# Pair 3 of a pooled attention kept in fp16 parts and transposed by DMA, with a new order of work

## The chip, the core and the metric

The kernel runs on one core of a Trainium2 chip. The metric is the device time in microseconds (us) of that core; three runs are shown for the kernel before, and their median is the figure that is forecast. TensorE's clock has two levels, 1.2 and 2.4 GHz; the profile gives the granted clock as a share of the upper one, so 0.50 is the lower level.

## The reference

The inputs q, k and v are (4 batches, 8 heads, 1152 rows, 64 columns), fp32, and the two weights are 512x2048 and 2048x512. Pooled attention comes first, then a feed-forward net with a squared ReLU:

```python
q_pool = q.reshape(B, H, S // 2, 2, D).mean(axis=3)          # 576 query rows
scores = scale * q_pool @ k.transpose(0, 1, 3, 2)            # 576 x 1152 per head
attn = exp(scores - max); attn = attn / (attn.sum(-1) + 1e-9)
x = (attn @ v).transpose(0, 2, 1, 3).reshape(2304, 512)
h = x @ w_in; g = relu(h) ** 2; out = g @ w_out              # fp32
```

## The kernel before

**Pairs and chunks.** Two heads make a pair; there are 16 pairs, four to a batch, so pairs 0 to 3 are batch 0. A pair has 9 chunks of 128 query rows, 144 chunks in all, numbered from 0. Pairs 2 and 3 are cut in two visits that alternate: chunks 18 to 21 and 26 to 30 are pair 2, chunks 22 to 25 and 31 to 35 are pair 3; pair 4 begins at chunk 36.

**The steps of a chunk i**, named as in the code: S.i are the scores (TensorE; lines 755 and 750 with fp16 parts, 734 in fp32), MX.i scales them and finds the row maximum (VectorE, DVE, line 766), MB.i forms the bias of the exponential, EX.i is the exponential with its row sum (ScalarE, ACT, line 790). Then the probabilities have to be transposed, in one of two ways:

- *fp32 by TensorE*: TP.i.x are three groups of three transposes through a PSUM bank (line 831), TC.i.x copies each group out (ACT line 841, or DVE line 843). The pair's values v are loaded as they are, and PV, the product with v, multiplies fp32 (line 942).
- *fp16 parts by DMA*: HI.i rounds to fp16 (ACT 794, DVE 798, POOL 363), LO.i is the rest (DVE or GpSimd, POOL, line 802), and TR.i is one transposing DMA for both parts (line 805, issued on SP's queue). The values are split too (VA and VD, DVE's part line 369), after a small Gram product GR and a norm GF that set their scale, and PV is 27 fp16 products for each head (line 950).

The setting FV lists the pairs of the first kind: 0, 1, 2 and 3 before.

**Preparing a pair n**: LK, LQ, LV (or LF, v as it is) load it on SP's queue; K and q are scaled and split (KA, KD, QA, QD) and transposed by DMA (KT line 628, QT line 641). QX.n.0 and QX.n.1 then copy the transposed q to the other half of the partitions (line 650, on DVE or POOL; a pair in the setting QXD has it moved by a plain DMA on SP's queue, line 647). Two raw buffers hold what is loaded.

**The feed-forward net.** Sixteen weight pieces are loaded (WL, UL), made into fp32 again (W0 to W5 and U0 to U5), and once the largest entry of w_out is known (US3.1, line 1316) split by WA (ACT, line 338), WB (ACT, line 1337) and WD (POOL, line 1341); for w_out these are UA, UB, UD. Nine blocks of 256 rows follow: RV, RB, XR divide by the row sums, XQ and XN find a norm, XA and XD split x (XA on ACT line 338, XD on DVE line 369), H.j.u are eight units of 24 matmuls with w_in (line 1114), HA, G1, G2, G3 the squared ReLU, O.j.t.d eight units of 12 matmuls with w_out (line 1163), OD and ST the output. The first block can begin as soon as batch 0's first rows have gone through PV.

**What sets the order.** Plan (line 50) takes every step with a fixed duration per engine, a priority (its place, plus an offset by kind from the tables off and off0 in CFG) and simulates five queues; the program is written out in the order that comes of it. Each engine, SP's queue too, then works its own list strictly in that order. So a step that waits holds up all that stands behind it on its engine.

Of the kernel before, what the change touches and what calls it, by code (L numbers as in the profile page):

```python
# [228 lines left out]
def kernel(  # L229
# [198 lines left out]
    def prep(n):  # L428
# [11 lines left out]
        def rk():  # L440
            return raw("k", n).rearrange("p (h c d) -> p h c d", h=2, c=9)
# [19 lines left out]
        if n == 0 and n in full_s:  # L461
            sk = k[b, 2 * hp : 2 * hp + 2].rearrange("h (p c) d -> p h (c d)", c=9)
            tk = rk

            def lk(o, x):
                nc.sync.dma_start(out=tk().rearrange("p h c d -> p h (c d)")[:, :, 192 * x : 192 * x + 192], in_=sk[:, :, 192 * x : 192 * x + 192])

            for x in range(3):
                add(("LK", n) + ((x,) if x < 2 else ()), {"SP": 900}, [], lambda o, x=x: lk(o, x), need, take=None if x else (("k", n), ("raw",), 0), after=[("LK", n, x - 1)] if x else prev)
        else:  # L470
            add(("LK", n), {"SP": 2500}, [], lambda o: load_kv(rk(), k), need, take=(("k", n), ("raw",), 0), after=prev)
        add(("LQ", n), {"SP": 2600}, [], load_q, need, take=(("q", n), ("raw",), 0), after=[("LK", n)])
# [980 lines left out]
```

## Time and the profile before

| | us |
|---|---|
| median of three runs | 796.63 (796.58 to 801.82) |
| the profiled execution, its own time | 804.16 |
| its span, first to last instruction | 802.3 |
| TensorE matmul busy in the span | 742.4 (93%) |
| DVE, ACT, POOL busy | 582.9 (73%), 575.4 (72%), 383.0 (48%) |
| mean granted TensorE clock | 0.977 |

The profiled execution is 7.5 us longer than the median; 1.9 us of its own time lie outside the span. A row of the list of groups reads: line, engine, operation, what it writes and reads with shape, count | busy us, mean ns of one | idle us of the engine before them and what ended it. A row of the timeline reads: start, us, engine, line, operation, count, and in brackets how long the engine had been idle and who released it. SPq is SP's queue: the time there is that of issuing a transfer, not of the transfer. Matmuls overlap, so the busy time of a group is less than count times mean.

### The profile page before, as it was taken

The page shows a single profiled execution, that of the slowest core. Times are in us where ns is not written, and L with a number is a line of the kernel's source. Part 1 is how long each engine was busy: PE and PEld are TensorE (multiplying, and loading weights), DVE is VectorE, ACT ScalarE, POOL GpSimd, SP SyncE. Part 2 cuts the span into 40 slices and gives each one's busy share as a digit, 9 for nine tenths or more (in the row PEclk, how much of TensorE's full clock was granted, in tenths as well). Part 3 has the DMA queues.
Part 4 walks back from the last instruction along what each step waited for, and adds up shares of the span by engine and source line. Part 5 has one row for each costly group of instructions (what it writes and reads, how often), then busy time and mean ns, then how long its engine had stood idle before and what let it go on. Part 6 is the DMA issues. An engine that isn't in the chain of part 4 may idle for free.

```text
span 802.3 us, 15287 instructions
## 1 busy us (share of the span) xinstructions
PE 742.4 (93%) x5998; PEld 491.7 (61%) x5998; DVE 582.9 (73%) x897; ACT 575.4 (72%) x894; POOL 383.0 (48%) x255
## 2 busy tenths in 40 slices
PE   4969788887899999998899999999999999999997
PEld 3546555544675577546666676577567657785654
DVE  3888999858799896888988899877888864202211
ACT  5776888778797888777897888788888854503412
POOL 2453633258676476365585656585666331001300
PEclk8888999999799999999999999999999999999999
DMA  8587383304999999999799999999999992000011
GB/s 285 207 218 214 119 239 136 75 9 90 219 187 202 192 227 210 211 209 183 159 212 210 207 207 208 211 201 213 204 209 199 182 189 46 1 1 14 14 27 27
DMA packets 324199, 127.77 MB, mean 159 GB/s; under 512 B 306976, under 2 KB 307744, under 8 KB 324128
## 3 DMA queue, kind: packets, MB, share of 16 engines
q1 hardware_dynamic: 324128, 126.80, 76.6%
q8 instruction: 47, 0.77, 0.4%
q14 instruction: 24, 0.20, 0.1%
HBM read 45.09 MB, written 4.72 MB: 62 GB/s over the span
## 4 chain that ended last, share of the span: by engine, by line
PE 42%; DVE 6%; DMA 4%; ACT 3%; issue 3%; POOL 1%; SPq 0%; ACTq 0%; DVEq 0%
PE ba L1163 9%; PE ba L1114 9%; PE bt L1163 6%; PE bt L1114 6%; PE s L755 5%; PE ba L950 5%; DVE s L766 2%; DMA PT<-buf 2%; DMA raw<-in_v_dram 1%; DVE region L1141 1%; ACT buf L794 1%; DMA kT<-buf 1%; PE s L750 1%; ACT buf L790 1%; DVE buf L802 1%
## 5 line engine op out<-in xcount | busy, mean ns | idle before, releaser
L766 DVE TENSOR_SCALAR_CACHE_REDUCE s<-s,esc 128x1152 f32<-128x1152 f32 x135 | 190.3, 1419 | 23.0 <-PE s L755 21.0
L1114 PEld LDWEIGHTS <-w 128*128 128x128 f16 x1728 | 169.1, 99 | 28.8 <-issue 3.2
L802 POOL TENSOR_TENSOR buf<-buf,buf 128x1152 f16<-128x1152 f32 x63 | 159.6, 2535 | 53.6 <-ACT buf L794 40.0
L790 ACT ACTIVATE buf<-s,ca 128x1152 f32<-128x1152 f32 x144 | 174.5, 1213 | 9.6 <-POOL ca L776 3.9
L755 PE MATMUL s<-kT,qT 128*128 128x512 f16 x720 | 136.6, 328 | 9.2 <-ACT buf L790 8.7
L1163 PE MATMUL ba<-w,region 128*128 128x512 f16 x624 | 142.3, 379 | 0.0
L1163 PEld LDWEIGHTS <-region 128*128 128x128 f16 x864 | 82.4, 98 | 95.6 <-issue 1.9
L1114 PE MATMUL ba<-region,w 128*128 128x256 f16 x1128 | 131.5, 274 | 1.2 <-DVE region L1041 0.5
L755 PEld LDWEIGHTS <-qT 128*128 128x128 f16 x720 | 64.0, 100 | 65.0 <-issue 16.5
L1141 POOL TENSOR_TENSOR region<-region 128x512 f16<-128x512 f32 x32 | 42.2, 1320 | 102.1 <-ACT region L1134 101.5
L950 PE MATMUL ba<-PT,v 128*64 128x320 f16 (+1 forms) x1296 | 84.7, 287 | 2.2 <-DMA PT<-buf 2.1
L794 ACT ACTIVATE buf<-buf 128x1152 f16<-128x1152 f32 x71 | 82.4, 1160 | 6.0 <-DMA PT<-buf 2.3
L950 PEld LDWEIGHTS <-v 128*64 128x64 f16 x1296 | 71.1, 110 | 15.0 <-issue 6.2
L802 DVE TENSOR_TENSOR buf<-buf,buf 128x1152 f16<-128x1152 f32 x45 | 67.5, 1501 | 16.2 <-ACT buf L794 11.6
L831 PE MATMUL ba<-ident,buf 128*128 128x128 f32 x324 | 51.6, 289 | 15.5 <-DVE PT L843 8.3
L1129 ACT ACTIVATE region<-region 128x512 f16<-128x512 f32 x72 | 45.0, 626 | 27.7 <-PE bt L1163 19.1
L1141 DVE TENSOR_TENSOR region<-region 128x512 f16<-128x512 f32 x40 | 39.1, 980 | 30.7 <-ACT region L1134 30.3
L831 PEld LDWEIGHTS ba<-ident,buf 128*128 128x128 f32 x324 | 35.2, 144 | 30.4 <-DVE PT L843 9.9
L1163 PE MATMUL bt<-w,region 128*128 128x512 f16 x240 | 52.6, 379 | 0.0
L1124 ACT ACTIVATE region<-ba 128x512 f32<-128x512 f32 x39 | 23.0, 591 | 36.8 <-PE ba L1114 36.8
L841 ACT ACTIVATE PT<-ba 128x384 f32<-128x384 f32 x74 | 34.0, 490 | 20.7 <-PE ba L831 20.0
L1114 PE MATMUL bt<-region,w 128*128 128x256 f16 x408 | 45.9, 273 | 0.0
(180 smaller groups left out, 993.9 us busy)
## 6 DMA issues: line engine op xcount, KB each, us to landing
raw<-in_q_dram SPq DMA_DIRECT2D x32, 288.0 KB, 3.7
raw<-in_k_dram SPq DMA_DIRECT2D x15, 576.0 KB, 4.6
region<-in_moe_w_in_dram SPq DMA_DIRECT2D x8, 1024.0 KB, 6.6
region<-in_moe_w_out_dram SPq DMA_DIRECT2D x8, 1024.0 KB, 5.3
raw<-in_v_dram SPq DMA_DIRECT2D x12, 576.0 KB, 4.7
out_dram<-half SPq DMA_DIRECT2D x20, 128.0 KB, 2.5
v<-in_v_dram SPq DMA_DIRECT2D x4, 576.0 KB, 7.1
out_dram<-buf SPq DMA_DIRECT2D x16, 128.0 KB, 2.4
```

Source lines behind the costliest of these rows:

```text
L755: nc.tensor.matmul(s[:, x, :w], lhsT=qt[:, l].rearrange("p c m -> p (c m)")[:, 128 * c0 + h : 128 * c0 + h + 255 : 2], rhs=rhs, **st)
L766: nc.vector.tensor_scalar(st3(), st3(), sc, 3e38, op0=ALU.mult, op1=ALU.min, accum_out=a[:, x : x + 1])
L790: nc.scalar.activation(P(), st3(), AF.Exp, bias=a[:, 1:2], scale=s1, accum_out=col)
L794: nc.scalar.activation(hl()[:, 0], P(), AF.Copy)
L802: e.tensor_tensor(out=hl()[:, 1], in0=P(), in1=hl()[:, 0], op=ALU.subtract)
L831: nc.tensor.matmul(t[:, y], lhsT=P()[:, c * 128 : (c + 1) * 128], rhs=ident, is_transpose=True, start=(y == 0), stop=(y == 2), skip_group_ ...
L841: nc.scalar.activation(out, t, AF.Copy)
L950: nc.tensor.matmul(px[h * 64 : (h + 1) * 64, 64 * r * (1 - h) : 64 * r * (1 - h) + N], lhsT=vv[:, h, kc, vl, :], rhs=p2(vi, r, h, 9 * pl + ...
L1114: nc.tensor.matmul(ph[:, f2], lhsT=w16[0][:, SLOT[f // 4], wl, a, f % 4 * 128 : (f % 4 + 1) * 128], rhs=xhl()[:, xl, a], start=(i == 0), s ...
L1129: nc.scalar.activation(gt[u][:, 0], rt[u % 2], AF.Square)
L1141: e.tensor_tensor(out=gt[u][:, 1], in0=rt[u % 2], in1=gt[u][:, 0], op=ALU.subtract)
L1163: nc.tensor.matmul(p[:, :DM], lhsT=g[:, gl, f % 2, tt * 128 : (tt + 1) * 128], rhs=w16[1][:, SLOT[f // 4], wl, f % 4], start=(f == 0 and g ...
```

## The change

FV loses pair 3, so pair 3 becomes one of the second kind: 27 TP and 27 TC go, and 9 HI, 9 LO, 9 TR, one VA, two VD, one GR, one GF come; LF.3 becomes LV.3, a load into a raw buffer. QXD, absent before, now lists pairs 1 to 4: their eight QX are plain DMAs. The fixed durations that Plan uses for SP's transfers and for LO on POOL are altered by up to 0.25 us each, and all offsets and slacks in CFG are new, so that every engine's list is in another order and some steps change their engine (KA is on POOL 9 times instead of 3, LO on POOL 70 times instead of 63, HI on ACT 87 times instead of 71).

```diff
-CFG = {'SPLIT': 0, 'TURN': [], 'TURNB': [], 'WDP': ((1, 0), (1, 1), (1, 2), (1, 3)), 'WSP': 0.3564, 'WOF': 20.8493, 'MSP': 9.2406, 'pen': 9140.9223, 'bl': 12.6041,
+CFG = {'SPLIT': 0, 'TURN': [], 'TURNB': [], 'WDP': ((1, 0), (1, 1), (1, 2), (1, 3)), 'WSP': 0.1233, 'WOF': 22.9195, 'MSP': 8.5588, 'pen': 10414.904, 'bl': 5.5869,
...
-'FV': (0, 1, 2, 3), 'FS': (0,), 'PART': 1,
+'FV': (0, 1, 2), 'FS': (0,), 'PART': 1, 'QXD': (1, 2, 3, 4),
...
-    ("WD", "DVE"): 2270, ("LO", "DVE"): 1285, ("LO", "POOL"): 2350, ("W4", "POOL"): 2120,
+    ("WD", "DVE"): 2270, ("LO", "DVE"): 1285, ("LO", "POOL"): 2420, ("W4", "POOL"): 2120,
...
-        add(("LQ", n), {"SP": 2600}, [], load_q, need, take=(("q", n), ("raw",), 0), after=[("LK", n)])
+        add(("LQ", n), {"SP": 2450}, [], load_q, need, take=(("q", n), ("raw",), 0), after=[("LK", n)])
...
-        add(("TR", i), {"SP": cfg("CTR", 2880)}, [("LO", i)] + ring, tr, i, give=("hl", i))
+        add(("TR", i), {"SP": cfg("CTR", 3010)}, [("LO", i)] + ring, tr, i, give=("hl", i))
```

**ACT's list up to XA.0**, the step that the first unit H.0.0 waits for. `w_1` and the scale `wS` are WA and WB of w_out, `PT<-ba` is TC, `s` the scores read by EX, `x_110` block 0. Before, the last twelve rows up to XA.0:

```order
L841 ACTIVATE PT<-ba_114 128x3x128
L1337 ACTIVATE region<-region,wS_1380 128x2048
L573 ACTIVATE buf_93,acc<-raw_101 128x576
L790 ACTIVATE buf_97,sums_87<-s_112,ca 128x1152
L794 ACTIVATE buf_96<-buf_97 128x1152
L338 ACTIVATE region<-ba_114 128x256
L338 ACTIVATE xm<-ba_114 64x64 x2
L338 ACTIVATE buf_93<-raw_101,psc 128x9x64
L338 ACTIVATE buf_95<-raw_102,psc 128x18x64
L1053 ACTIVATE half_100<-region 128x1024
L790 ACTIVATE buf_99,sums_87<-s_113,ca 128x1152
L338 ACTIVATE buf_97<-x_110,xs 128x1024
```

And now, from XQ of the same block to XA.0:

```order
L1053 ACTIVATE half_100<-x_110 128x1024
L790 ACTIVATE buf_95,sums_86<-s_112,ca 128x1152
L794 ACTIVATE buf_96<-buf_95 128x1152
L338 ACTIVATE w_1_91<-w_1_91,wS_1350 128x2048
L1337 ACTIVATE w_1_91<-w_1_91,wS_1350 128x2048
L338 ACTIVATE v_0_107<-raw_102,psc 128x18x64
L773 ACTIVATE ca<-ca,cols 128x1
L790 ACTIVATE buf_95,sums_86<-s_113,ca 128x1152
L794 ACTIVATE buf_97<-buf_95 128x1152
L338 ACTIVATE w_1_91<-region,wS_1350 128x2048
L338 ACTIVATE buf_99<-x_110,xs 128x1024
```

XA.0 now stands behind EX.35 and ahead of the last WB; before it stood behind EX.39, pair 4's fourth chunk, and behind the split of pair 5's q and K (the rows that read raw_101 and raw_102 with psc).

**SP's queue around the loads of pairs 4 and 5.** `raw<-in_q`, `in_k`, `in_v` are LQ, LK, LV, `qT` and `kT` QT and KT, `PT<-buf` a TR. Before, from LV.4 on:

```order
L450 DMA raw_101<-in_v_dram 128x2x576
L450 DMA raw_102<-in_k_dram 128x2x576
L641 DMA_TRANSPOSE qT_105<-half_100 128x9x128
L628 DMA_TRANSPOSE kT_103<-buf_99 128x18x128
L458 DMA raw_101<-in_q_dram 64x1152 x2
L805 DMA_TRANSPOSE PT<-buf_98 128x18x128
L805 DMA_TRANSPOSE PT<-buf_94 128x18x128
```

And now, from LQ.4 on:

```order
L458 DMA raw_102<-in_q_dram 64x1152 x2
L805 DMA_TRANSPOSE PT<-buf_96 128x18x128
L805 DMA_TRANSPOSE PT<-buf_97 128x18x128
L805 DMA_TRANSPOSE PT<-buf_95 128x18x128
L805 DMA_TRANSPOSE PT<-buf_94 128x18x128
L641 DMA_TRANSPOSE qT_105<-half_100 128x9x128
L450 DMA raw_102<-in_v_dram 128x2x576
L647 DMA qT_105<-qT_105 64x1152 x2
L450 DMA raw_101<-in_k_dram 128x2x576
L628 DMA_TRANSPOSE kT_103<-buf_96 128x18x128
L805 DMA_TRANSPOSE PT<-buf_99 128x18x128
```

QT.4, LV.4, QX.4, LK.5 and KT.4 now stand behind TR.22 to TR.25, pair 3's first four; QX.4 is on this queue and waits there for QT.4 to land.

## Rows read from the trace of the kernel before

**Rows 1.** Busy us by engine in five stretches, then clock, DMA share, GB/s.
```profile
core 0: us, PE busy (x) PEld busy (x) DVE busy (x) ACT busy (x) POOL busy (x), PEclk, DMA share, GB/s
0.00:80.00 80.00, 60.36 (x444) 41.16 (x445) 55.79 (x92) 53.50 (x85) 33.48 (x27) 0.87 0.76 231
80.00:157.00 77.00, 64.60 (x528) 42.61 (x528) 74.50 (x114) 63.86 (x101) 31.45 (x20) 1.00 0.51 149
157.00:206.50 49.50, 37.69 (x270) 21.59 (x267) 35.06 (x66) 40.19 (x53) 33.05 (x16) 0.89 0.35 67
206.50:660.00 453.50, 442.04 (x3760) 294.56 (x3761) 385.90 (x566) 371.23 (x586) 272.46 (x178) 0.99 1.07 202
660.00:802.00 142.00, 137.70 (x1006) 91.82 (x1004) 31.69 (x61) 46.66 (x75) 12.60 (x14) 1.00 0.10 21
```

**Rows 2.** The chain that ended last, a late piece.
```profile
787.34 10.37 PE bt L1163 x48
```

**Rows 3.** The list of groups: TensorE.
```profile
L831 PE MATMUL ba<-ident,buf 128*128 128x128 f32 x324 | 51.6, 289 | 15.5 <-DVE PT L843 8.3 <-ACT PT L841 4.8 <-ACT buf L790 1.9
L942 PE MATMUL ba<-PT,v 128*64 128x256 f32 (+1 forms) x288 | 38.4, 422 | 2.9 <-DVE x L1041 1.6 <-DVE wsc L1291 1.0
L950 PE MATMUL ba<-PT,v 128*64 128x320 f16 (+1 forms) x1296 | 84.7, 287 | 2.2 <-DMA PT<-buf 2.1
L547 PE MATMUL ba<-raw 128*128 128x128 bf16 x81 | 6.9, 236 | 6.8 <-DMA raw<-in_k_dram 6.4 <-ACT PT L841 0.5
```

**Rows 4.** The list of groups: ACT, DVE and POOL.
```profile
L841 ACT ACTIVATE PT<-ba 128x384 f32<-128x384 f32 x74 | 34.0, 490 | 20.7 <-PE ba L831 20.0
L843 DVE COPY PT<-ba 128x384 f32<-128x384 f32 x34 | 17.8, 551 | 2.2 <-PE ba L831 2.1
L794 ACT ACTIVATE buf<-buf 128x1152 f16<-128x1152 f32 x71 | 82.4, 1160 | 6.0 <-DMA PT<-buf 2.3 <-DMA kT<-buf 1.1
L802 POOL TENSOR_TENSOR buf<-buf,buf 128x1152 f16<-128x1152 f32 x63 | 159.6, 2535 | 53.6 <-ACT buf L794 40.0 <-DMA raw<-in_q_dram 5.7 <-issue 2.7
L802 DVE TENSOR_TENSOR buf<-buf,buf 128x1152 f16<-128x1152 f32 x45 | 67.5, 1501 | 16.2 <-ACT buf L794 11.6 <-POOL buf L802 2.4 <-POOL buf L363 1.5
L369 DVE SCALAR_TENSOR_TENSOR v<-raw,psc,v 128x576 f16<-128x576 f32 x24 | 36.3, 1518 | 0.5 <-POOL v L340 0.2
L650 DVE COPY qT<-qT 64x1152 f16<-64x1152 f16 x14 | 12.0, 860 | 2.7 <-DMA qT<-half 2.4
L766 DVE TENSOR_SCALAR_CACHE_REDUCE s<-s,esc 128x1152 f32<-128x1152 f32 x135 | 190.3, 1419 | 23.0 <-PE s L755 21.0 <-ACT buf L794 0.9 <-PE s L750 0.3
L790 ACT ACTIVATE buf<-s,ca 128x1152 f32<-128x1152 f32 x144 | 174.5, 1213 | 9.6 <-POOL ca L776 3.9 <-DVE s L766 2.9 <-DMA PT<-buf 0.9
```

**Rows 5.** Timeline of TensorE: the first H units.
```profile
206.56 4.05 PE L1114 MATMUL ba<-buf,w 128*128 128x256 f16 x24
...
211.43 5.40 PE L1114 MATMUL ba<-buf,w 128*128 128x256 f16 x48
```

**Rows 6.** Timeline of DVE and ACT: US3.1's end, UA.1.0, XA.0.
```profile
156.86 0.13 DVE L1316 TENSOR_SCALAR wsc<-wS 128x1 f32<-128x1 f32 x1
...
157.08 1.99 ACT L338 ACTIVATE w<-w,wS 128x2048 f16<-128x2048 f32 x1
...
198.55 1.15 ACT L338 ACTIVATE buf<-x,xs 128x1024 f16<-128x1024 f32 x1 [0.28 <-DVE xs L1082]
```

**Rows 7.** As rows 1, the stretch ahead of the first H.
```profile
192.00:208.00 16.00, 8.59 (x61) 4.75 (x58) 13.11 (x28) 12.04 (x19) 13.04 (x8) 0.72 0.96 177
```

**Rows 8.** Line 805 on SP's queue; a KT there; the S that followed.
```profile
L805 SPq DMA_TRANSPOSE PT<-buf x108: 2377/2858/4211, 192.8 to 660.4; - x108
...
493.64 4.15 SPq L628 DMA_TRANSPOSE kT<-buf  x1
...
501.40 1.14 PE L755 MATMUL s<-kT,qT 128*128 128x512 f16 x6 [0.26 <-DMA kT<-buf]
```

**Rows 9.** Timeline of DVE: a split beside an LO on POOL.
```profile
200.46 2.57 DVE L369 SCALAR_TENSOR_TENSOR buf<-raw,psc,buf 128x576 f16<-128x576 f32 x1
```

More of the change, by code (lines that the diff above doesn't have):

```diff
@@ L470, in prep @@
         else:
-            add(("LK", n), {"SP": 2500}, [], lambda o: load_kv(rk(), k), need, take=(("k", n), ("raw",), 0), after=prev)
-        add(("LQ", n), {"SP": 2600}, [], load_q, need, take=(("q", n), ("raw",), 0), after=[("LK", n)])
+            add(("LK", n), {"SP": 2350}, [], lambda o: load_kv(rk(), k), need, take=(("k", n), ("raw",), 0), after=prev)
+        add(("LQ", n), {"SP": 2450}, [], load_q, need, take=(("q", n), ("raw",), 0), after=[("LK", n)])
         if n in full_v:
-            add(("LF", n), {"SP": 2200}, oldv, lambda o: load_kv(v4(slot), v), visits[vs[0]][2], after=[("LQ", n)])
+            add(("LF", n), {"SP": 2250}, oldv, lambda o: load_kv(v4(slot), v), visits[vs[0]][2], after=[("LQ", n)])
         else:
-            add(("LV", n), {"SP": 2200}, [], lambda o: load_kv(rv(), v), need, take=(("v", n), ("raw",), 0), after=[("LQ", n)])
+            add(("LV", n), {"SP": 2250}, [], lambda o: load_kv(rv(), v), need, take=(("v", n), ("raw",), 0), after=[("LQ", n)])
         def qsum(o):
@@ L674, in prep @@
                 add(K + (h,), {"POOL": 1250} if kbp else {"DVE": 730}, [("KB" if kbp else "KA", n)] + ([K + (0,)] if h else []), lambda o, h=h: (kg if kbp else kd)(o, h), need, give=("k", n) if h else None)
-            add(("KT", n), {"SP": 2550}, [K + (1,)] + old, kt, need, give=("k2", n), take=(("kT", n), ("buf",), cfg("RK", 2)) if keep else None)
+            add(("KT", n), {"SP": 2700}, [K + (1,)] + old, kt, need, give=("k2", n), take=(("kT", n), ("buf",), cfg("RK", 2)) if keep else None)
             add(("QA", n), alt("QA", ACT=600, POOL=700), [("GS", n, "qk"), ("QS", n)] , qa, need, take=qt_)
             add(("QD", n), {"DVE": 760}, [("QA", n)], qd, need, give=("q", n))
-            add(("QT", n), {"SP": 1450}, [("QD", n)] + old, qt, need, give=("q2", n), take=(("qT", n), ("buf",), cfg("RK", 2)) if keep else None)
+            add(("QT", n), {"SP": 1550}, [("QD", n)] + old, qt, need, give=("q2", n), take=(("qT", n), ("buf",), cfg("RK", 2)) if keep else None)
             for z in range(2):
@@ L1189, in block @@
             add(("OD", j, tt), {"DVE": 720}, [("O", j, tt, 3), ("XO", j)], od, at + 12 + 4 * tt, take=(("o", j, tt), ("buf", "half"), cfg("RO", 1)), give=("O", j, tt, 0))
-            add(("ST", j, tt), {"SP": 1400}, [("OD", j, tt)], st, at + 12 + 4 * tt, give=("o", j, tt))
+            add(("ST", j, tt), {"SP": 1300}, [("OD", j, tt)], st, at + 12 + 4 * tt, give=("o", j, tt))
     ring2 = {}
```

2 lines of the change are left out of this document (1 added, 1 removed).

## The prediction

> **What bounds the kernel now.** I read the busy time by stretch first. From 206.5 to 660 us TensorE is busy 442.0 of 453.5 us, and after that 137.7 of 142 [rows 1]; the chain that ended last consists there of H and O units back to back [rows 2]. From the first H unit at 206.56 us on [rows 5] the kernel is therefore a fixed amount of matmul work, and what counts is when that stage begins and how much is done by then. Ahead of it TensorE idles 19.6, 12.4 and 11.8 us in the first three stretches, 43.8 us together, and another engine limits: DVE is busy 74.5 of 77 us from 80 to 157, and from 157 to 206.5 no engine is above 81% (ACT 40.2 of 49.5), so there it is chains [rows 1]. DMA is nearly idle in that third stretch (0.35), while its share is above 1 later.
>
> The groups show what a transpose costs in either way: transposes by TensorE take 51.6 us for 324, 0.159 each, and copies of 0.49 to 0.55 us behind each three [rows 3, 4]; by DMA a chunk takes 2.86 us of SP's queue [rows 8], a rounding of 1.16 and a rest of 1.5 (DVE) or 2.5 us (POOL) [rows 4].
>
> **What the change removes and adds, all of it ahead of 206.5 us.**
>
> TensorE: 81 transposes go, 81 x 0.159 = 12.9 us. PV of pair 3 goes from a quarter of 38.4 to a twelfth of 84.7 us, 9.6 to 7.1, so 2.5 less. Nine Gram products more are 6.9 x 9 / 81 = 0.8, and two small norm products about 0.3 (an estimate, of the Gram's own size each) [rows 3]. Net **-14.3 us**. All of it lies where TensorE is not the limit, so it counts only as far as the first H unit comes earlier.
>
> DVE up to US3.1, the scale of w_out, which ends at 157.0 [rows 6] and closes DVE's full stretch. In its list 126 steps stand ahead of US3.1 now, 134 before. By kind: six TC copies less (6 x 0.551 = 3.3), three QX less (3 x 0.86 = 2.6), two MX less (2 x 1.42 = 2.8); two VD more (2 x 1.52 = 3.0), one LO more (1.5) [rows 4]; the rest nearly cancels (about +0.5, an estimate). Sum -3.7, so 153.3 us. Beside it POOL now works three LO there (3 x 2.535 = 7.6 us [rows 4]). The trace has a DVE split of 2.57 us beside such an LO [rows 9] against a mean of 1.52 for its kind [rows 4]: about 1 us for each LO met, so +3, between 0 and 7.6. US3.1 then ends at 156 (153 to 161).
>
> The Trainium skill, "Advanced Engine Details and Errata", VectorE Performance Modes, says that the second Vector SBUF port is shared with GpSimd, so that such instructions block each other; that speaks against giving POOL seven LO more. Were the block complete, the sum would take the upper end, 161; the row shows about 1 us each.
>
> ACT from UA.1.0 to the start of XA.0: before 198.55 - 157.08 = 41.5 us [rows 6]. The list now holds four UA and three UB of 1.99 (13.9), five EX of 1.21 (6.1), three HI of 1.16 (3.5), three TC of 0.49 (1.5), and QK, VA, XQ and two MB (about 4.5, by the 1.2 us of EX for the first three) [rows 4, 6]: 29.5 us. At the busy share of that stretch, 81% [rows 1], that is 36 us, so XA.0 starts at 156 + 36 = 192 instead of 198.6. The three UD between (POOL, in a chain with UA and UB) were hidden in the 41.5 us before; if POOL's LO.32 and LO.33 hold them up, 2 x 2.5 = 5 us come on top. From XA.0's start to the first H it took 8.0 us [rows 5, 6], of which XA is 1.15; XD waited behind the 2.57 us split [rows 9]. I take 4, between 2.5 and 8. That gives 196. The other way to count goes by the steps ahead of H.0.0 in the lists: DVE has 162 ahead of XD.0 instead of 177, by the same prices 11 us less (four MX, four TC, three QX, two KD among what goes; two LO, two VD among what comes), TensorE 158 units instead of 194. 11 us off 206.56 is 195.6; at DVE's busy share there, 71% [rows 1], it is 15 us and 191. I take **194** for H.0.0, between 188 and 205.
>
> From there TensorE should be full. Up to S.42 its list holds H.0.0 to H.0.2 at 2.70 each (5.40 / 2 [rows 5]), five S of about 1.0, one PV of 3.5 (84.7 / 24 [rows 3]) and two small products (0.6): 17.3 us, so 211.3. The kernel before reaches the same state, three H and all S up to 42, at 211.43 + 5.40 = 216.8 less the one S.43 between, 215.8 us (its first H at the lower clock, 4.05 instead of 2.70 us [rows 5], is in that). So 4.5 us earlier, but with an XN and half an RB still to do that were done before, 1 us: **-3.5 us**. Put shortly, the gain is 197.5 less the time of H.0.0: the new list wants H.0.0 five chunks earlier, and at 206.56 as before it would be 9 us slower.
>
> In the full stage the lists run alike: at S.60 there are 21 feed-forward units ahead instead of 17, at S.78 34 in both, at S.141 91 instead of 90. Since TensorE is full in between, a lead there neither adds nor takes. The eight QX by DMA are hidden in DMA's slack; if not, each holds SP's queue until QT has landed, some 3 us where the next load waits, at pair 1 and pair 4 at most.
>
> Transposes by DMA are also what the Trainium skill, "VectorE: DVE Perf Modes", Rules for kernel authors, advises against where PSUM will do; its table of transpose paths gives 1309 ns for one 128x128 by DMA and 390 by TensorE, which would be 9 x 18 x 1.309 = 212 us of queue (an estimate by that page). Here 18 such tiles take 2.86 us [rows 8], so the trace disagrees and decides: 9 x 2.86 = 26 us, where DMA had nothing to do.
>
> The sum is made against the profiled execution: 804.2 - 3.5 = 800.7. Against the median, 7.5 us lower, 796.6 - 3.5 = **793.1**.
>
> **The rivals.**
>
> *The freed TensorE time counts in full* (faster). Then the 14.3 us come off, and the gap ahead of the first H closes as well: in 192 to 208 TensorE is busy 8.6 of 16 us [rows 7], 7.4 idle. -21.7, **774.9**. For it: DVE and ACT both have less to do ahead of H.0.0, and no engine is full after 157. Against it: DVE is at 97% from 80 to 157 and loses under 4 us. Chance 0.22.
>
> *The first H is no earlier* (same or slower). LO blocks DVE wholly, which is 4.6 us over the forecast, and LO.32 and LO.33 delay UD by 5 more: H.0.0 at 202 to 206.5, and all of S.38 and on stands behind it in TensorE's list. 796.6 + 4.5 to 9: **801 to 806**. For it: POOL is the one engine with much more to do ahead of H.0.0. Against it: it is busy 33.1 of 49.5 us there. Chance 0.10.
>
> *K comes late at the pair boundaries* (slower). Before, the transposes of K for pairs 5 to 15 stood ahead of 4 to 10, in the mean 7.1, of the previous pair's TR on SP's queue; now of 4 to 8, in the mean 5.9, and for pairs 5, 6, 10, 12 and 13 of only 4 or 5. With 5 ahead the trace has K issued at 493.64 and the S that needs it starting at 501.40, the moment K lands, with TensorE 0.26 us idle [rows 8]: no slack was left. If each of the five comes one TR later, 5 x 2.86 = 14.3 us of TensorE idle in the full stage, one for one: 796.6 - 3.5 + 14.3 = **807**. It decides when these waits sum to more than 3.5 us; 12 make it slower by over 1%. For it: KA is on POOL for nine pairs instead of three, behind LO of 2.5 us. Against it: pairs 12 and 13 stood at 5 and 4 before and cost 0.3 us. Chance 0.16.
>
> **How the numbers follow.** The forecast has 0.52, with its own range 787 to 800 (H.0.0 at 188 to 201). What can be told from no change here is about 1%, 8 us: below 788.7 or above 804.6. The forecast gives 0.11 faster, for H.0.0 before 189.5, and 0.41 same; the first rival 0.22 faster; the second 0.06 same and 0.04 slower; the third 0.04 same and 0.12 slower. Faster 0.33, same 0.51, slower 0.16. The range 777 to 805 leaves out the fastest part of the first rival (0.06) and most of the third (0.12).
>
> **What would show it.** US3.1 near 156, XA.0 near 191, the first H near 194, S.42 and three H done near 211; from there to the end as many us as before, within 3. Right is also: TensorE busy near 728 us, DMA no longer idle from 157 to 190. Wrong it is if the first H comes before 188 or after 201, if TensorE's idle time after that exceeds 16 us, if waits for K or for PT before an S or PV sum to over 4 us, or if the granted clock is 0.50 for long stretches of chunks 22 to 35, where TensorE has the least to do.

## The result, and the profile after

The changed kernel takes 807.09 us, the median of 12 runs (802.64 to 809.13); the kernel before took 801.56 in 12 runs on the same chip (796.17 to 803.42). The ratio is 1.0076, with a 95% interval of 1.0050 to 1.0102: slower by 0.8%, 5.5 us by the medians, where 3.5 us less were forecast. That is inside the 1% which the prediction called no change, but the interval leaves out 1. The median of three runs on which the forecast of 793.1 stood was also 4.9 us below that of the 12, so of the 14.0 us between forecast and time 4.9 belong to the base and 9.0 to the sum; the range ended at 805. The profiled execution of the changed kernel has 806.63 us and a span of 804.8, the one before 804.16 and 802.3: between the two traces 2.5 us have to be explained. The other 3.0 lie between traces and medians and can't be read from a trace.

The busy time by stretch, in the columns of [rows 1]; the last stretch ends at 804.8:

```profile
0.00:80.00 80.00, 60.47 (x458) 40.41 (x459) 58.57 (x91) 55.64 (x88) 34.33 (x28) 0.94 0.80 256
80.00:157.00 77.00, 60.38 (x485) 38.78 (x484) 73.43 (x107) 56.39 (x84) 35.66 (x22) 0.93 0.64 157
157.00:206.50 49.50, 38.15 (x301) 24.71 (x298) 44.66 (x75) 47.45 (x59) 35.44 (x18) 0.90 0.70 120
206.50:660.00 453.50, 436.56 (x3712) 289.40 (x3709) 389.90 (x575) 368.07 (x576) 284.07 (x181) 0.98 1.08 203
660.00:804.80 144.80, 140.18 (x1022) 92.95 (x1016) 33.28 (x64) 51.92 (x83) 3.38 (x6) 1.00 0.12 24
```

From 157 to 206.5 DVE has 9.6 us more work than in [rows 1] and ACT 7.3 more, in the same time. From 206.5 on TensorE idles 16.9 + 4.6 = 21.5 us, where it was 11.5 + 4.3 = 15.8. Over the whole span it is busy 735.7 us instead of 742.4, DVE 599.8 instead of 582.9, POOL 392.9 instead of 383.0.

The groups that answer to [rows 3, 4], of the changed kernel:

```profile
L831 PE MATMUL ba<-ident,buf 128*128 128x128 f32 x243 | 39.6, 291 | 15.2 <-DVE PT L843 5.7 <-ACT PT L841 3.8 <-ACT buf L790 2.4
L942 PE MATMUL ba<-PT,v 128*64 128x256 f32 (+1 forms) x216 | 27.5, 408 | 0.4 <-ACT PT L841 0.3
L950 PE MATMUL ba<-PT,v 128*64 128x256 f16 (+1 forms) x1404 | 93.0, 290 | 1.5 <-DMA PT<-buf 1.5
L794 ACT ACTIVATE buf<-buf 128x1152 f16<-128x1152 f32 x87 | 101.0, 1160 | 4.1 <-DMA PT<-buf 1.3
L802 POOL TENSOR_TENSOR buf<-buf,buf 128x1152 f16<-128x1152 f32 x70 | 175.8, 2514 | 42.4 <-ACT buf L794 33.6 <-DVE buf L798 3.6 <-issue 2.5
```

The transposes by TensorE are down by 12.0 us (81 fewer), PV by 10.9 - 8.3 = 2.6: both as forecast. TensorE's waits from 206.5 on, of the changed kernel (who waited, for whom, us, times, longest):

```profile
PE s L755 <- ACT buf L790: 7.0, 11, 1.8
...
PE ba L950 <- DMA PT<-buf: 1.5, 1, 1.5
```

and of the kernel before, the same view:

```profile
PE s L755 <- ACT buf L790: 3.1, 4, 1.4
PE ba L950 <- DMA PT<-buf: 2.1, 2, 1.5
```

S waits more for the exponential of two chunks earlier. No S waits for K.

**Where the lead was, and where it went.** TensorE around the first H units, the changed kernel's timeline:

```profile
187.00 1.01 PE L1114 MATMUL ba<-buf,w 128*128 128x256 f16 x4 [0.29 <-ACT buf L338]
189.21 4.27 PE L1114 MATMUL ba<-buf,w 128*128 128x256 f16 x20 [1.19 <-DVE buf L369]
...
195.27 2.78 PE L1114 MATMUL ba<-buf,w 128*128 128x256 f16 x24
...
203.96 2.78 PE L1114 MATMUL ba<-buf,w 128*128 128x256 f16 x24
...
207.01 1.17 PE L750 MATMUL s<-kT,qT 128*64 128x512 f16 x12
```

H.0.0 starts at 187.0, its second part, which needs XD, at 189.2; S.42 (line 750) and three H are done at 208.2. The kernel before was there at 215.8, 7.6 us later. Further on I count in TensorE's own order: the time at which an S starts, and what was done by then. A feed-forward unit counts 2.65 us, a step of PV (54 products, line 950) 3.5 us. The rows of S.68, S.74 and S.80, the kernel before (the first row is S.67 and S.68 together, so S.68 starts at 324.3):

```profile
323.38 2.11 PE L755 MATMUL s<-kT,qT 128*128 128x512 f16 x12
...
351.13 1.15 PE L755 MATMUL s<-kT,qT 128*128 128x512 f16 x6
...
381.99 1.14 PE L755 MATMUL s<-kT,qT 128*128 128x512 f16 x6
```

and of S.68 and S.80 in the changed kernel (its S.74, at 357.39, is in a fence below):

```profile
327.27 1.14 PE L755 MATMUL s<-kT,qT 128*128 128x512 f16 x6
...
380.57 1.14 PE L755 MATMUL s<-kT,qT 128*128 128x512 f16 x6 [0.36 <-ACT buf L790]
```

At S.60 (285.3 before, 288.6 now) the changed list has 21 units behind it instead of 17: 10.6 - 3.3, 7.3 us ahead. At S.68 it has 30 instead of 26, but one PV of the pairs from 4 on less (5 instead of 6): 10.6 - 3.5 - 3.0, 4.1 us ahead. At S.72 (340.1 and 348.0) it has 32 units instead of 29 and as many PV, and the lead is gone. At S.74 both have 32, and it is 6.3 us behind; at S.80 it has 35 units instead of 37: 1.4 - 5.3, 3.9 us behind. So 10.4 us went from S.68 to S.74, ahead of H.2.0, and 2.4 came back by S.80: 8.0 us in the twelve chunks. From S.60 to S.68 3.2 us go as well in this trace, and behind S.80 1.4 come back. The stretch in three pieces, cut where MX.68, MX.72, MX.76 and MX.80 start on DVE, the kernel before:

```profile
328.20:342.80 14.60, 14.60 (x125) 8.11 (x125) 12.65 (x17) 9.88 (x17) 4.28 (x3) 1.00 1.09 207
342.80:365.60 22.80, 18.89 (x151) 10.95 (x150) 17.42 (x38) 18.03 (x27) 12.80 (x10) 0.94 1.06 196
365.60:386.50 20.90, 20.25 (x199) 16.10 (x197) 19.97 (x30) 15.30 (x25) 11.44 (x8) 0.99 1.06 205
```

and the changed kernel:

```profile
328.40:349.20 20.80, 18.79 (x170) 11.81 (x171) 13.34 (x22) 14.11 (x22) 9.40 (x6) 0.92 1.06 209
349.20:366.60 17.40, 11.68 (x91) 7.42 (x91) 14.96 (x30) 13.68 (x22) 12.42 (x9) 0.80 1.08 195
366.60:383.10 16.50, 15.02 (x153) 11.08 (x150) 13.81 (x25) 15.91 (x26) 14.79 (x10) 1.00 1.19 214
```

From S.68 to S.80 TensorE's list has eleven units and two PV before, five units and three PV now: 15.9 - 3.5, 12.4 us less, but the stretch is only 4.4 us shorter (53.3 instead of 57.7). In the pieces above TensorE idles 9.2 us instead of 4.6, and its granted clock, between its two levels, falls to 0.80 in the middle: the 162 products of PV there keep it busy for 12.8 us instead of 10.5, those of S for 12.3 instead of 11.3. With a higher clock the stretch is no shorter: the run below with shorter H units in blocks 3 and 4, up to S.90 the same program, takes 53.4 us from S.68 to S.80 at a clock of 0.94, and TensorE idles 10.8 us of it. Blocks 0 and 1 have 32 units; the changed list has worked off the last of them ahead of S.71, and the next, H.2.0, stands behind S.74 and needs block 2 first: PV.9.0, RB.2, XR, XQ.2, XN.2, XA.2, XD.2. What ran meanwhile shows in the chain of the changed kernel (start, us, what):

```profile
333.88 1.17 ACT buf L794
...
335.12 2.37 POOL buf L802
...
338.61 4.60 DMA PT<-buf
...
343.26 4.80 PE ba L950 x53
348.06 1.10 PE s L755 x6
...
350.67 0.60 DVE region L1041 x2
...
352.61 1.40 DVE s L766 x2
...
354.23 0.77 ACT buf L573 x2
...
356.59 1.77 POOL buf L340
...
360.08 1.48 DVE s L766 x2
```

It goes from the rounding (ACT) over LO (POOL) and its transpose to PV.9.0, and then through XR, a maximum, the norm of the next q and its KA: of some 28 us TensorE has 6.5. ACT and TensorE in the middle of it, from the timeline:

```profile
351.83 1.06 ACT L1053 ACTIVATE half<-region 128x1024 bf16<-128x1024 f32 x1 [0.87 <-DVE region L1041]
...
354.99 1.15 ACT L338 ACTIVATE region<-region,xs 128x1024 f16<-128x1024 f32 x1
...
356.04 1.20 ACT L790 ACTIVATE buf<-s,ca 128x1152 f32<-128x1152 f32 x1
...
357.39 2.08 PE L755 MATMUL s<-kT,qT 128*128 128x512 f16 x6 [1.75 <-ACT buf L790]
```

EX.72 (356.04) stands on ACT's list behind XQ.2 and XA.2, and S.74 waits for it.

### The profile page after: what moved, and what is told of

Same layout as the page of the kernel before. It is cut to its first block, busy times and chain, and to the rows that moved or that the text cites. A ratio compares the mean times of both kernels' runs of the same rounds, so it can differ in the third digit from the quotient of the medians.

```text
span 804.8 us, 15253 instructions
## 1 busy us (share of the span) xinstructions
PE 735.7 (91%) x5964; PEld 486.3 (60%) x5964; DVE 599.8 (75%) x906; ACT 579.5 (72%) x888; POOL 392.9 (49%) x255
## 4 chain that ended last, share of the span: by engine, by line
PE 64%; DVE 14%; ACT 9%; DMA 5%; issue 4%; POOL 1%; SPq 1%; DVEq 0%; ACTq 0%; POOLq 0%
PE ba L1163 15%; PE ba L1114 12%; PE s L755 10%; PE ba L950 9%; PE bt L1114 7%; PE bt L1163 5%; DVE s L766 5%; ACT buf L790 4%; DMA region<-in_moe_w_in_dram 2%; DMA PT<-buf 2%; PE ba L831 1%; PE ba L942 1%; DVE v L369 1%; PE s L750 1%; PE s L734 1%
## 5 line engine op out<-in xcount | busy, mean ns | idle before, releaser
L802 POOL TENSOR_TENSOR buf<-buf,buf 128x1152 f16<-128x1152 f32 x70 | 175.8, 2514 | 42.4 <-ACT buf L794 33.6
L790 ACT ACTIVATE buf<-s,ca 128x1152 f32<-128x1152 f32 x144 | 174.6, 1214 | 16.9 <-POOL ca L776 6.1
L755 PE MATMUL s<-kT,qT 128*128 128x512 f16 x720 | 140.4, 334 | 18.0 <-ACT buf L790 17.2
L1163 PE MATMUL ba<-w,region 128*128 128x512 f16 x672 | 153.0, 379 | 0.0
L794 ACT ACTIVATE buf<-buf 128x1152 f16<-128x1152 f32 x87 | 101.0, 1160 | 4.1 <-DMA PT<-buf 1.3
L950 PE MATMUL ba<-PT,v 128*64 128x256 f16 (+1 forms) x1404 | 93.0, 290 | 1.5 <-DMA PT<-buf 1.5
L802 DVE TENSOR_TENSOR buf<-buf,buf 128x1152 f16<-128x1152 f32 x47 | 70.6, 1503 | 15.8 <-ACT buf L794 14.0
L1124 ACT ACTIVATE region<-bt 128x512 f32<-128x512 f32 x20 | 11.9, 597 | 60.3 <-PE bt L1114 60.3
L1114 PE MATMUL bt<-region,w 128*128 128x256 f16 x480 | 54.2, 273 | 0.0
L831 PE MATMUL ba<-ident,buf 128*128 128x128 f32 x243 | 39.6, 291 | 15.2 <-DVE PT L843 5.7
L773 ACT ACTIVATE ca<-ca,cols 128x1 f32<-128x1 f32 x71 | 20.6, 290 | 38.9 <-DVE s L766 38.0
L369 DVE SCALAR_TENSOR_TENSOR buf<-raw,psc,buf 128x576 f16<-128x576 f32 x35 | 44.0, 1258 | 1.8 <-POOL buf L340 1.8
L831 PEld LDWEIGHTS ba<-ident,buf 128*128 128x128 f32 x243 | 26.5, 145 | 27.4 <-DVE PT L843 8.6
```

What stands on the lines that cost most here:

```text
L369: nc.vector.scalar_tensor_tensor(out=o, in0=x, scalar=s, in1=h, op0=ALU.mult, op1=ALU.subtract)
L755: nc.tensor.matmul(s[:, x, :w], lhsT=qt[:, l].rearrange("p c m -> p (c m)")[:, 128 * c0 + h : 128 * c0 + h + 255 : 2], rhs=rhs, **st)
L790: nc.scalar.activation(P(), st3(), AF.Exp, bias=a[:, 1:2], scale=s1, accum_out=col)
L794: nc.scalar.activation(hl()[:, 0], P(), AF.Copy)
L802: e.tensor_tensor(out=hl()[:, 1], in0=P(), in1=hl()[:, 0], op=ALU.subtract)
L831: nc.tensor.matmul(t[:, y], lhsT=P()[:, c * 128 : (c + 1) * 128], rhs=ident, is_transpose=True, start=(y == 0), stop=(y == 2), skip_group_ ...
```

## The experiments

All fifteen are timed in turn with the kernel before on the same chip, so their ratios to it can be compared; a difference of two such ratios is uncertain by about 0.4%, 3 us. Theory A: the lead is lost ahead of H.2.0, where TensorE does not set the pace, and behind it TensorE does. The rivals are F (TensorE is full throughout, as the prediction had it), B (the transposes by DMA set the pace), C (POOL slows DVE), D (the swaps of q on SP's queue), G (DVE) and H (several engines stand at the same height).

**TensorE's work, ahead of the hole and behind it.** In the first the list is (0, 1), in the second (3, 4):

```diff
-  (wl, xl, a) for wl, xl in ((0, 0), (0, 1), (1, 0)) for a in range(KD)
+  ts = ((0, 0), (0, 1)) if m in (0, 1) else ((0, 0), (0, 1), (1, 0))
+  (wl, xl, a) for wl, xl in ts for a in range(KD)
```

> The 16 H units of the first two blocks of the feed-forward part leave out the product with the second half of w_in: 16 x 8 = 128 matmuls of 0.273 us less than the changed kernel, about 35 us of TensorE less by the count of matmuls at that duration, all between S.36 and S.66. Theory A (block 2's start eats the lead): TensorE time saved ahead of S.71 only lengthens the hole ahead of H.2.0, where the changed kernel has no feed-forward unit left: 2 to 8 us of it come out, 799 to 805. Theory F (TensorE is full from the first H unit on, as the prediction had it): nearly all of it comes out, below 780. Theory B (the transposes by DMA set the pace, 4.33 us for each of 108 chunks): nothing, 805 to 808.

> The same products are left out in the 16 H units of blocks 3 and 4, between S.90 and S.130, behind the hole: again 128 matmuls of 0.273 us, 35 us, less than the changed kernel. Theory A: behind H.2.0 TensorE has feed-forward units enough, so at least 25 of the 35 us come out: 772 to 782. Theory F: the same as for the first two blocks. Theory B: the 108 transposes still take 468 us from 194 on and their end at 663 is followed by the same 140 us of feed-forward units: 803 to 808.

The 35 us were a misreading: 0.273 us is how long one product takes, and they overlap; 1728 of them keep TensorE busy for 195.0 us, 0.113 each, so 14.4 us were taken out. Measured: 803.69 us, ratio 1.0018 (0.9989 to 1.0047), 4.6 us less than the changed kernel; and 808.15, 1.0082 (1.0051 to 1.0114), nothing. Scaled to 14.4 us, F and A's second half asked for about 14 and 10. F falls, and so does A's second half. The first is in A's range, but it can't be read from its trace where the 4.6 us came out: the profiled execution, 808.82, is the slowest of the twelve. From MX.88 to MX.128, where blocks 3 and 4 have their H units, the changed kernel reads

```profile
421.70:601.20 179.50, 175.53 (x1455) 115.32 (x1455) 159.86 (x234) 143.72 (x227) 104.30 (x73) 1.00 1.05 203
```

and the second run, over the same chunks,

```profile
419.70:600.20 180.50, 166.97 (x1327) 104.18 (x1327) 158.60 (x234) 142.46 (x227) 104.65 (x73) 0.98 1.06 202
```

TensorE goes from 98% to 93% busy, and the stretch takes as long.

**The transposes, and the swaps of q.**

```diff
+ if i >= 45:
+     nc.sync.dma_start_transpose(out=pslot(vi, j, False)[:, :9], in_=hl()[:, 0])
```

> From chunk 45 on only the fp16 upper part of P is transposed (half of each transpose is left out, the lower part of PT stays what it was), nothing else is changed. Theory B: the transposes were 2.86 us of the queue each; 99 chunks at half of that free over 100 us of DMA, and the time falls by 15 us or more, below 790. Theories A and F: TensorE or the chains between the engines set the pace, and only the one wait for PT (1.5 us) goes: 803 to 808.

Measured: 804.62, 1.0022 (0.9994 to 1.0050), 4.3 us less. DMA's share falls from 1.1 to 0.7, and the gain is a third of the least that B asked for. B falls as the only bound.

```diff
- nc.sync.dma_start(out=t[a : a + 64, 1], in_=t[b_ : b_ + 64, 0])
+ nc.vector.tensor_copy(t[a : a + 64, 1], t[b_ : b_ + 64, 0])
```

> The eight swaps of q of pairs 1 to 4 are copied by DVE at the place where the changed kernel has a DMA for them, all else as in the changed kernel. Theory D (the swaps by DMA hold SP's queue while they wait for the transposed q, and by that all that follows): 2 to 8 us less, 799 to 805. Theories A, B and F: the swaps are hidden either way: 805 to 809; DVE gets 8 x 0.86 us more ahead of S.48, most of it where DVE is not the limit.

Measured: 809.52, 1.0092 (1.0061 to 1.0123), 1.3 us more: the swaps by DMA cost nothing. D falls.

**DVE and POOL.** LO returns at once from chunk 45 on where its engine is DVE, then POOL, then either:

```diff
+ if i >= 45 and o["eng"] in ("DVE",):
+     return
```

> As the run with half transposes, and from chunk 45 on the lower part of P is not computed where DVE would do it: 40 LO of 1.48 us, 59 us of DVE less. Theory G (from S.40 to S.143 it is DVE that sets the pace of 4.41 us a chunk, whatever TensorE and DMA do): at least 20 us come out, below 785. Theory F (TensorE is full): nothing against half transposes, 801 to 806. Theory H (no engine alone: the four lists wait for each other in turn, and work taken from one gives a small part of it back): 3 to 12 us, 792 to 801.

> As the run with half transposes, and from chunk 45 on the lower part of P is not computed where POOL would do it: 59 LO of 2.51 us, 148 us of POOL less, and DVE is freed of what these LO block. Theory C (POOL's work slows DVE, and that is what the changed kernel lost): 8 us or more come out, below 796. Theory F: nothing, 801 to 806. Theory H: 3 to 12 us. POOL alone, at 0.6 busy, is not the limit in any theory.

> As the run with half transposes, and from chunk 45 on no lower part of P is computed at all. If TensorE sets the pace (F) the time stays at 801 to 806 with DVE, POOL and DMA all much less busy; if DVE and POOL do (G and C together), below 770, and then TensorE, 92 units and 98 chunks of S and PV from S.45 on, is the next limit.

Measured: 798.99, 0.9955 (0.9927 to 0.9983); 800.22, 0.9956 (0.9924 to 0.9989); 797.66, 0.9930 (0.9903 to 0.9957). Against the half transposes that is 5.4, 5.3 and 7.4 us for 59, 148 and 207 us of work. G and C fall as the only bound; what came is H's 3 to 12. The same stretch from MX.88 to MX.128 of the third run,

```profile
418.90:594.40 175.50, 174.97 (x1455) 115.01 (x1453) 114.52 (x214) 143.44 (x225) 46.58 (x53) 1.00 0.71 141
```

has TensorE alone at its limit, all but 0.5 us busy, and that is worth no more than 4 us of 179.5.

```diff
  def ka(o):
+     o["eng"] = "ACT" if n >= 4 else o["eng"]
```

> The upper half of K of pairs 5 and 8 to 14 is rounded by ACT (1.16 us each) instead of POOL at the same places; the order is the changed kernel's. Theory C: eight KA less on POOL beside DVE's work, and K earlier: 3 to 8 us less than the changed kernel, 799 to 804. Theories F and H: within 2 us of it, 805 to 809; ACT has 9 us more, where S already waits for EX, and that can cost up to 5: 812.

Measured: 807.97, 1.0072 (1.0038 to 1.0105), within 0.3 us of the changed kernel. KA on POOL is not what cost.

**Units moved out of the hole and into it.** put(x, y) takes the step x from its place in the order that the planner found and puts it right behind y; all else keeps its place.

```diff
+ put(("O", 1, 1, 1), ("O", 1, 1, 0))
+ put(("O", 1, 1, 2), ("S", 70))
+ put(("O", 1, 1, 3), ("PV", 9, 0))
```

> The kernel before, its order kept but for the last three O units of block 1: they stand right behind O.1.1.0, S.70 and PV.9.0 instead of behind S.72 and S.73, so that its list has no feed-forward unit from S.71 to H.2.0, as the changed kernel's has. Theory A (a lead in feed-forward units is lost where they run out ahead of H.2.0): TensorE idles 5 to 8 us more between S.71 and H.2.0, and the end comes 3 to 7 us later than before: 805 to 809. Theory F (TensorE is full, the place of a unit does not matter): within 1 us of before, 801 to 803.

Measured: 807.50, 1.0058 (1.0029 to 1.0086), 4.7 us more, as A has it. The kernel before, with no other change than three units done a little earlier, becomes as slow as the changed one within 2 us. From MX.68 to MX.80 its trace has 61.5 us instead of 58.3 for the same work, and TensorE idles 8.2 us instead of 4.6: 3.6 more, not 5 to 8. From MX.72 to MX.76, ahead of H.2.0, its trace looks like the changed kernel's, with the clock down and 6 us idle:

```profile
349.70:369.60 19.90, 13.70 (x129) 9.12 (x129) 18.14 (x40) 17.08 (x25) 12.53 (x9) 0.83 0.86 170
```

```diff
+ put(("RB", 2, 1), ("XR", 2, 0)); put(("O", 1, 1, 2), ("RB", 2, 1)); put(("O", 1, 1, 3), ("XN", 2))
+ put(("OD", 1, 1), ("XD", 2)); put(("RV", 3), ("OD", 1, 1)); put(("ST", 1, 1), ("RV", 3))
+ put(("RT", 3), ("S", 74)); put(("RU", 3), ("RT", 3))
+ for x in ("RB", 2, 0), ("GF", 9, "qk"): plan.slot[x] = ("a", 1)
```

> The changed kernel, its order kept but for O.1.1.2 and O.1.1.3, which stand behind RB.2.1 and XN.2 in the hole ahead of H.2.0 instead of ahead of PV.8.1 and S.71; what reads or reuses their bank (OD, ST, RV.3, RT.3, RU.3) follows them. Theory A: the two units (5.3 us) fill TensorE's idle time there, and all that stands ahead comes as much earlier: 3 to 6 us less than the changed kernel, 801 to 804. Theory F: within 1 us of it, 806 to 808. Theory H (no engine alone): 0 to 2 us less.

Measured: 812.77, 1.0121 (1.0094 to 1.0148), 3.6 us more: a miss. From MX.68 to MX.72 it reads

```profile
328.90:350.10 21.20, 15.37 (x145) 11.03 (x146) 11.79 (x20) 13.96 (x22) 10.03 (x6) 0.76 1.07 212
```

against 20.80 in the changed kernel: with two units fewer these four chunks take as long, so TensorE is not the limit from S.68 on, and not only from S.71. The units then stand ahead of XN.2 and GF.9, on which the chain above depends; that this is why it got slower is an argument, and no run shows it.

**Both limits lifted.** No LO from chunk 45 on, and the shorter H units besides, in blocks 3 and 4 and then in 0 and 1.

> As the run without any lower part of P from chunk 45 on (797.7), and the product with the second half of w_in is left out in blocks 3 and 4: 128 matmuls of 0.113 us (195.0 us for 1728 in the changed kernel's profile; the 0.273 used for the earlier runs is the time of one, and they overlap), 14.4 us. With DVE, POOL and DMA at 0.3 to 0.75 busy, TensorE is alone at the limit behind H.2.0: theory H gives 10 to 14 us, 784 to 788, though the same cut brought nothing with the lower parts in place. If it brings nothing here either, a chain that none of the theories has sets the pace.

> The same as the run before in this list, but the products are left out in blocks 0 and 1, ahead of the hole. Theory A: the units only run out earlier, and 1 to 5 of the 14.4 us come out, 793 to 797. Theory F: 14 us, 783 to 785, as in blocks 3 and 4.

Measured: 789.33, 0.9821 (0.9788 to 0.9854), 8.7 us less than without LO alone; and 795.83, 0.9917 (0.9884 to 0.9949), 1.0 us less. The same cut that brought nothing in blocks 3 and 4 brings 8.7 of its 14.4 us once DVE, POOL and DMA have room; H had asked for 10 to 14. In blocks 0 and 1 it brings next to nothing, as A has it, but not for A's reason. From MX.42 to MX.68, where those units are, the run without LO alone reads

```profile
213.00:326.90 113.90, 111.98 (x909) 73.25 (x907) 79.01 (x135) 95.01 (x149) 40.38 (x35) 1.00 0.82 164
```

and the one with the cut

```profile
216.90:329.40 112.50, 105.02 (x807) 65.85 (x806) 76.25 (x135) 94.57 (x149) 39.18 (x35) 0.97 0.82 165
```

The stretch is 1.4 us shorter, and TensorE idles 7.5 us of it instead of 1.9. The saving was gone by S.68 already, so this run does not test what happens ahead of H.2.0; it shows that TensorE was not the only limit before that either. The cut in blocks 3 and 4, from MX.88 to MX.128:

```profile
412.80:581.10 168.30, 163.49 (x1326) 103.09 (x1324) 113.99 (x213) 142.49 (x225) 46.99 (x53) 0.99 0.73 147
```

**TensorE's work added.** Three H units are done twice, which adds 8 us:

```diff
- for f2 in range(2):
+ for f2 in (0, 1, 0, 1) if m == 0 and 3 <= u < 6 else (0, 1):
```

> The changed kernel with H.0.3, H.0.4 and H.0.5 done twice (the same products again, 72 matmuls of 0.113 us, 8 us more on TensorE between S.42 and S.45): its lead of three units is taken away. Theory A (between S.68 and S.80 TensorE is not the limit and what lead there is gets lost): 0 to 4 us more than the changed kernel, 807 to 811. Theory F (TensorE is full from the first H unit on): all 8 us, 813 to 816.

> The changed kernel with H.3.3 to H.3.5 done twice, 8 us more on TensorE between S.97 and S.100, behind the hole. Theories A and F: 6 to 9 us more than the changed kernel, 812 to 816, since there TensorE stands at the limit together with the others. If it is below 810, TensorE has slack there too.

> The kernel before with H.0.3 to H.0.5 done twice. It has no lead to lose, 11 units in S.68 to S.80 and less idle time there. Theory A: 4 to 8 us more than before, 806 to 810, more than the same edit costs the changed kernel. Theory F: 8 us, as in the changed kernel.

Measured: 817.02, 1.0190 (1.0152 to 1.0228), 9.1 us more than the changed kernel; 816.98, 1.0190 (1.0159 to 1.0221), 9.1 more; 810.24, 1.0121 (1.0090 to 1.0153), 9.7 more than before. A missed the first and the third: it had asked for less than 8 us in the changed kernel and for more in the kernel before than in the changed one, and F's 8 us came in all three, as nearly as these ratios tell. In the first, S.80 starts 6.0 us later than in the changed kernel (386.6 and 380.6), and the twelve chunks from MX.68 to MX.80 take 56.9 us, no less than the 54.7 of the changed kernel: the delay came through. My reading afterwards, which no run tests: the edit does not take away the lead, since the doubled units hold up S.44 and all behind it on every engine, while a unit done early costs its 2.65 us at once, and that comes back only where a chunk without a unit is shorter by as much.

## Why the prediction was wrong

**Right: the early stage, its end if not its steps.** US3.1 ended at 157 as before (156 forecast; DVE had 132.0 us of work up to there instead of 130.3, where the sum had 3.7 less, and 3 more for POOL's). XA.0 started at 185.8 (192): 28.8 us after US3.1, the 29.5 us of ACT's work without the waits that I had added. H.0.0 started at 187.0, in full at 189.2 (194), S.42 and three H were done at 208.2 (211.3). So the lead at that point was 7.6 us instead of 4.5 less the 1 us of XN and RB: the part with the most working erred by 3 us, on the safe side.

**Right in kind, missed in sum: TensorE's work.** 12.0 us of transposes and 2.6 of PV went, as priced, but busy time fell by 6.7 and not 14.3. S of line 755 went from 136.6 to 140.4 us at 720 products each, some of it at the lower clock around 350 us.

**Wrong: "From there TensorE should be full", and with it "a lead there neither adds nor takes" and "from there to the end as many us as before".** From S.42 and three H to the end the changed kernel takes 804.8 - 208.2 = 596.6 us; before it was 802.3 - 215.8 = 586.5. That is 10.1 us more, the whole lead and 2.5 on top, and 8.0 us go in S.68 to S.80. I had read a busy share of 97% [rows 1] as a bound and taken the count of units at S.60 (21 against 17) for harmless. But those units cost TensorE's time before S.68, where the changed kernel arrives 3.0 us later, and were to be paid back behind it. There the chain through ACT, POOL, DMA and DVE sets the time, and the work that was no longer to be done became idle time. That the place of units alone costs time there, the move of three of them in the kernel before shows, at 4.7 us. That it is the cause of all 8.0 us in the changed kernel is not shown: two units moved back made it 3.6 us slower. That TensorE is no bound by itself in the stage called full, the cuts show: 14.4 us less work brought 4.6 us ahead of H.2.0 and nothing behind it.

**The range and the rivals.** The prediction named two signs of being wrong that came: idle time above 16 us behind the first H (21.5) and a first H ahead of 188. No rival had this mechanism. The third gave 807, which is the time that came, but its cause did not: no S waited for K, and PT cost one wait of 1.5 us.

**The freed TensorE time in full (774.9)** fell with the same cuts.

**Open.** Which of the waits between S.68 and S.80 would have to go for the lead to hold: all LO gone shortens that stretch only from 54.7 to 52.0 us (MX.68 to MX.80). Why moving units back into the gap made it worse. Why the medians lie 5.5 us apart and the two traces 2.5. And what the new order and pair 3's new path cost or bring separately: the order is found for the whole list at once, and with either part alone it would be another one, so that wasn't run. No run that does all the work was faster than the kernel before.

## What to carry to other kernels

A busy share near 1 over a long stretch does not make an engine the bound: add work to it and take work away, since here 8 us more cost 9 to 10 us in each place tried and 14 us less brought 0 to 5. Where independent work fills the gaps of a chain, count not only how much of it is done at a point but how much is left for the next place at which the chain alone sets the pace, and ask what becomes available there.

## What the runs showed of the hardware

The prediction took 1 us for a DVE step beside a long one on POOL, between 0 and a complete block. In the changed kernel such steps waited the other one out:

```profile
167.50 1.42 DVE L766 TENSOR_SCALAR_CACHE_REDUCE s<-s,esc 128x1152 f32<-128x1152 f32 x1
167.87 2.37 POOL L802 TENSOR_TENSOR buf<-buf,buf 128x1152 f16<-128x1152 f32 x1
...
171.28 4.09 POOL L1341 TENSOR_TENSOR w<-w 128x2048 f16<-128x2048 f32 x1 [0.68 <-ACT w L1337]
...
172.43 3.56 DVE L798 CAST buf<-buf 128x1152 f16<-128x1152 f32 x1 [0.52 <-ACT buf L790]
...
179.81 4.06 POOL L1341 TENSOR_TENSOR w<-w 128x2048 f16<-128x2048 f32 x1 [0.31 <-ACT w L1337]
...
180.85 3.64 DVE L369 SCALAR_TENSOR_TENSOR v<-raw,psc,v 128x576 f16<-128x576 f32 x1
```

The rounding on DVE ends 0.6 us after POOL's step, and a split behind it likewise: 3.56 and 3.64 us, where the same kernel's 18 roundings on DVE have a median of 0.76 and the next split, at 184.49, takes 0.79. The maximum at 167.50, beside an LO, keeps its 1.42 us: it is not every DVE step that is held. The split of [rows 9], which I had read as about 1 us more, has the same end: its LO on POOL ran to 202.42 in that trace, and the split ended 0.6 us later, at 203.03. The Trainium skill, "Advanced Engine Details and Errata", VectorE Performance Modes, says that GpSimd and DVE steps that use the shared port block each other; these two rows agree with a complete block, which I had given the end of the range. What it cost here no run shows; the stage came early all the same.
